# Decode attention on one core: softmax stages regrouped, and the scaled negative maximum moved from GpSimd to ScalarE

## The chip, the core and the metric

One Trainium2 chip, one core of it. The metric is the device time of one launch in microseconds (us); lower is better. The kernel before takes 512.92 us in the median of its first 5 runs (510.8 to 516.18). A run more than 1.5% above the fastest run of the same kernel counts as slow; everything compared below is fast unless said otherwise. Engines are named as the profile has them: PE (TensorE), DVE (VectorE), ACT (ScalarE), POOL (GpSimd), SP (SyncE, which here only issues DMAs).

## The reference

```python
B, H, Sq, Sk, D = 1, 16, 1, 8192, 256          # bf16 q, k, v
def reference(q, k, v):
    scale = q.shape[-1] ** -0.5
    scores = jnp.einsum("bhqd,bhkd->bhqk", q, k) * scale
    p = softmax(scores, axis=-1)
    return jnp.einsum("bhqk,bhkd->bhqd", p, v)
```

There is one query row per head. Each head reads 4 MiB of K and 4 MiB of V once, 134 MB in all, and does very little arithmetic on them.

## The kernel before

A head's 8192 keys lie on 128 partitions, 64 chunks each. K comes in 4 tiles of 16 chunks (1 MiB each), and so does V; 8 buffers for each, all issued from one queue. For each K tile, VectorE multiplies 7 chunks by q in one instruction and ScalarE sums them; the other 9 chunks VectorE multiplies and sums itself. Then comes the softmax over the head, and PE multiplies by V one head later.

```python
for h in range(H):
    for t in range(NKT):                        # 4 tiles of a head
        kt = kpool.tile([P, C, D], BF16, name="kt")
        k_eng.dma_start(out=kt, in_=kh[:, t * C : (t + 1) * C, :])
        nc.vector.tensor_tensor(out=prod[:], in0=kt[:, 0:BC, :], in1=..., op=ALU.mult)   # BC = 7
        for c in range(BC):                     # ScalarE sums a chunk
            nc.scalar.activation(out=junk, in_=prod[:, c, :], func=ACT.Copy,
                                 accum_out=scores[:, n0 + c : n0 + c + 1])
        for c in range(BC, C):                  # VectorE: multiply and sum a chunk
            nc.vector.tensor_tensor_reduce(out=scratch, in0=kt[:, c, :], in1=q_bc[:, h, :], ...,
                                           accum_out=scores[:, n : n + 1])
    nc.vector.tensor_reduce(out=rowmax, in_=scores, axis=AX.X, op=ALU.max)
    nc.gpsimd.partition_all_reduce(gmax, rowmax, channels=P, reduce_op=bass_isa.ReduceOp.max)
    nc.gpsimd.tensor_scalar(out=negbias, in0=gmax, scalar1=-scale, scalar2=None, op0=ALU.mult)
    nc.scalar.activation(out=p_h, in_=scores, func=ACT.Exp, bias=negbias, scale=scale,
                         accum_out=rowsum)
    nc.gpsimd.partition_all_reduce(den, rowsum, channels=P, reduce_op=bass_isa.ReduceOp.add)
    nc.vector.reciprocal(out=rden[0:1, :], in_=den[0:1, :])
    ...                                         # V loads, PE and scaling of the head before
```

The framework's scheduler orders the instructions of each engine when the program is built. In the traces an engine does not pass over one that waits: in the kernel before, VectorE is idle for 16.08 us before the reciprocal at 225.77 us, although the reductions behind it belong to a K tile whose multiply had already run at 208.26. So where an instruction stands on its engine has to be read from the built program, not from the source.

Of the kernel before, what the change touches and what calls it, by code (L numbers as in the profile page):

```python
# [8 lines left out]
FP32 = mybir.dt.float32  # L9
BF16 = mybir.dt.bfloat16  # L10
ACT = mybir.ActivationFunctionType
ALU = mybir.AluOpType
AX = mybir.AxisListType
# [3 lines left out]
def kernel(  # L17
# [7 lines left out]
    nc = tc.nc  # L25
    P = nc.NUM_PARTITIONS

    B, H, SQ, D = q.shape
# [3 lines left out]
    NCH = SK // P  # L32
    scale = float(D) ** -0.5

    C = min(int(os.environ.get("KC", "16")), NCH)
    VC = min(int(os.environ.get("VC", str(C))), NCH)
    assert NCH % C == 0 and NCH % VC == 0
    NKT = NCH // C
    NVT = NCH // VC
    BC_LIST = [int(x) for x in os.environ.get("BC", "7").split(",")]  # L40
# [2 lines left out]
    v_eng_name = os.environ.get("VENG", "sync")  # L43
    k_eng_name = os.environ.get("KENG", "sync")
    R = int(os.environ.get("RETIME", "2"))
    JUNK_PSUM = os.environ.get("JUNK_PSUM", "0") == "1"
    NORM_ENG = os.environ.get("NORM_ENG", "scalar")
    VLAG = int(os.environ.get("VLAG", "1"))
    QSPLIT = os.environ.get("QSPLIT", "1") == "1"

    q_flat = q.rearrange("b h q d -> (b h q d)")
    out_flat = out.rearrange("b h q d -> (b q) (h d)")

    consts = ctx.enter_context(tc.tile_pool(name="consts", bufs=1))
# [1 line left out]
    vpool = ctx.enter_context(tc.tile_pool(name="vpool", bufs=vbufs))  # L56
    ppool = ctx.enter_context(tc.tile_pool(name="ppool", bufs=3))
    junkp = ctx.enter_context(tc.tile_pool(name="junkp", bufs=2))
    small = ctx.enter_context(tc.tile_pool(name="small", bufs=6))
    spool = ctx.enter_context(tc.tile_pool(name="spool", bufs=5))  # L60
    scratch_pool = ctx.enter_context(tc.tile_pool(name="scratchp", bufs=2))
    psum_o = ctx.enter_context(tc.tile_pool(name="psum_o", bufs=R + 1, space=bass.MemoryType.PSUM))
    if JUNK_PSUM:
        psum_j = ctx.enter_context(tc.tile_pool(name="psum_j", bufs=2, space=bass.MemoryType.PSUM))

    v_eng = getattr(nc, v_eng_name)
    k_eng = getattr(nc, k_eng_name)
    norm_eng = getattr(nc, NORM_ENG)

    q_bc = consts.tile([P, H, D], BF16, name="q_bc")  # L70
    if QSPLIT:
        q2 = q.rearrange("b h q d -> (b q) h d")
        nc.sync.dma_start(out=q_bc[:, 0:1, :], in_=q2[:, 0:1, :].partition_broadcast(P))
        nc.gpsimd.dma_start(out=q_bc[:, 1:, :], in_=q2[:, 1:, :].partition_broadcast(P))  # L74
    else:
        nc.sync.dma_start(out=q_bc, in_=q_flat.partition_broadcast(P))

    ostage = consts.tile([1, H * D], BF16, name="ostage")

    o_tiles = {}  # L80
    p_tiles = {}
    rden_tiles = {}
    v_tiles = {}

    def issue_v(hh):
        vhh = v[0, hh].rearrange("(p n) d -> p n d", p=P)
        tiles = []
        for t in range(NVT):
            vt = vpool.tile([P, VC, D], BF16, name="vt")
            v_eng.dma_start(out=vt, in_=vhh[:, t * VC : (t + 1) * VC, :])  # L90
            tiles.append(vt)
        v_tiles[hh] = tiles

    def emit_norm(hh):
        o_ps = o_tiles.pop(hh)
        rden = rden_tiles.pop(hh)
        if NORM_ENG == "scalar":
            nc.scalar.activation(  # L98
                out=ostage[:, hh * D : (hh + 1) * D],
                in_=o_ps,  # L100
                func=ACT.Copy,
                scale=rden[0:1, 0:1],
            )
        else:
            nc.vector.tensor_scalar_mul(
                out=ostage[:, hh * D : (hh + 1) * D], in0=o_ps, scalar1=rden[0:1, 0:1]
            )

    for h in range(H):
        kh = k[0, h].rearrange("(p n) d -> p n d", p=P)  # L110
        vh = v[0, h].rearrange("(p n) d -> p n d", p=P)

        scores = spool.tile([P, NCH], FP32, name="scores")
        if VLAG == 0:
            pending_v_issue = h
        else:
            pending_v_issue = None
        for t in range(NKT):
            BC = min(BC_LIST[(h * NKT + t) % len(BC_LIST)], C)
            kt = kpool.tile([P, C, D], BF16, name="kt")  # L120
            k_eng.dma_start(out=kt, in_=kh[:, t * C : (t + 1) * C, :])  # L121
            n0 = t * C
            if BC > 0:
                prod = ppool.tile([P, BC, D], BF16, name="prod")
                nc.vector.tensor_tensor(  # L125
                    out=prod[:],
                    in0=kt[:, 0:BC, :],
                    in1=q_bc[:, h : h + 1, :].to_broadcast([P, BC, D]),
                    op=ALU.mult,
                )  # L130
                for c in range(BC):
                    if JUNK_PSUM:
                        junk = psum_j.tile([P, D], BF16, name="junkps")
                    else:
                        junk = junkp.tile([P, D], BF16, name="junk")
                    nc.scalar.activation(  # L136
                        out=junk,
                        in_=prod[:, c, :],
                        func=ACT.Copy,
                        accum_out=scores[:, n0 + c : n0 + c + 1],  # L140
                    )
            for c in range(BC, C):
                n = n0 + c
                scratch = scratch_pool.tile([P, D], BF16, name="scratch")
                nc.vector.tensor_tensor_reduce(  # L145
                    out=scratch,
                    in0=kt[:, c, :],
                    in1=q_bc[:, h, :],
                    scale=1.0,
                    scalar=0.0,  # L150
                    op0=ALU.mult,
                    op1=ALU.add,
                    accum_out=scores[:, n : n + 1],
                )

        rowmax = small.tile([P, 1], FP32, name="rowmax")
        nc.vector.tensor_reduce(out=rowmax, in_=scores, axis=AX.X, op=ALU.max)  # L157
        gmax = small.tile([P, 1], FP32, name="gmax")
        nc.gpsimd.partition_all_reduce(gmax, rowmax, channels=P, reduce_op=bass_isa.ReduceOp.max)  # L159
        negbias = small.tile([P, 1], FP32, name="negbias")  # L160
        nc.gpsimd.tensor_scalar(  # L161
            out=negbias, in0=gmax, scalar1=-scale, scalar2=None, op0=ALU.mult
        )

        p_h = spool.tile([P, NCH], BF16, name="p_h")
        rowsum = small.tile([P, 1], FP32, name="rowsum")
        nc.scalar.activation(  # L167
            out=p_h,
            in_=scores,
            func=ACT.Exp,  # L170
            bias=negbias,
            scale=scale,
            accum_out=rowsum,
        )
        den = small.tile([P, 1], FP32, name="den")
        nc.gpsimd.partition_all_reduce(den, rowsum, channels=P, reduce_op=bass_isa.ReduceOp.add)  # L176
        rden = small.tile([P, 1], FP32, name="rden")
        nc.vector.reciprocal(out=rden[0:1, :], in_=den[0:1, :])  # L178
        rden_tiles[h] = rden

        if VLAG == 0:
            issue_v(h)
        elif h - VLAG >= 0:
            issue_v(h - VLAG)

        def emit_pv(hp):
            o_ps = psum_o.tile([1, D], FP32, name="o_ps")
            o_tiles[hp] = o_ps
            p_use = p_tiles.pop(hp)
            tiles = v_tiles.pop(hp)  # L190
            for t in range(NVT):
                vt = tiles[t]
                for c in range(VC):
                    n = t * VC + c
                    nc.tensor.matmul(  # L195
                        out=o_ps,
                        lhsT=p_use[:, n : n + 1],
                        rhs=vt[:, c, :],
                        start=(n == 0),
                        stop=(n == NCH - 1),  # L200
                    )

        p_tiles[h] = p_h
        if VLAG == 0:
            emit_pv(h)
        elif h - VLAG >= 0:
            emit_pv(h - VLAG)

        if h - R - VLAG >= 0:
            emit_norm(h - R - VLAG)  # L210

    for hh in sorted(list(p_tiles.keys())):
        issue_v(hh)
        o_ps = psum_o.tile([1, D], FP32, name="o_ps")
        o_tiles[hh] = o_ps
        p_use = p_tiles.pop(hh)
        tiles = v_tiles.pop(hh)
        for t in range(NVT):
            vt = tiles[t]
            for c in range(VC):  # L220
                n = t * VC + c
                nc.tensor.matmul(  # L222
                    out=o_ps,
                    lhsT=p_use[:, n : n + 1],
                    rhs=vt[:, c, :],
                    start=(n == 0),
                    stop=(n == NCH - 1),
                )
    for hh in sorted(list(o_tiles.keys())):
        emit_norm(hh)  # L230

    nc.sync.dma_start(out=out_flat, in_=ostage)

# [29 lines left out]
```

## Time and profile before

| | before |
|---|---|
| time, median | 512.92 us |
| busy: DVE / ACT / PE / POOL | 53% / 39% / 29% / 6% |
| mean DMA rate over the span (first to last instruction) / from 12.76 to 90 us | 266 / 421 GB/s |
| DVE idle, waiting for `den` | 224.6 us in 16 waits |

The page's engine line, and its rows of 40 equal slices of the span (one digit is a busy share in tenths; GB/s is what the DMA engines moved), of the kernel before:

```profile
PE 150.1 (29%) x1024; PEld 99.1 (19%) x1024; DVE 269.1 (53%) x1248; ACT 196.5 (39%) x945; POOL 28.3 (6%) x53
...
DVE  3998272480934808439075191661925709357440
...
DMA  8999999986593874928839469284692864971000
GB/s 299 424 420 422 417 422 423 369 310 281 173 406 121 313 306 164 378 117 298 361 123 365 170 253 405 92 358 209 222 421 98 315 262 168 402 258 80 0 0 2
```

No engine is busy all the time. DMA is full from the second slice to the eighth and ragged after that, so something stops feeding it. The waits view (who waited for whom: total us, number of waits, longest) of the kernel before names it:

```profile
DVE rden L178 <- POOL den L176: 224.6, 16, 16.1
ACT p_h L167 <- POOL negbias L161: 190.4, 16, 15.5
...
POOL negbias L161 <- issue: 170.2, 16, 13.5
...
DVE prod L125 <- DMA kt<-in_k_dram: 8.8, 2, 8.3
```

VectorE loses 224.6 us, 14 us per head, to one 1x1 reciprocal, because its instructions run in order: everything behind the reciprocal waits too. It hardly ever waits for K (8.8 us, of which 8.3 at the start). Here is one head in the timeline of the kernel before (start, duration, engine, line, operation; in brackets the idle time of the engine and what ended it), cut to the softmax chain:

```profile
204.01 0.22 DVE L157 TENSOR_REDUCE rowmax<-scores 128x1 f32<-128x64 f32 x1
...
204.34 1.13 POOL L159 PARTITION_ALL_REDUCE gmax<-rowmax  x1 [11.60 <-DVE rowmax L157]
...
216.43 0.26 POOL L161 TENSOR_SCALAR negbias<-gmax 128x1 f32<-128x1 f32 x1 [10.97 <-issue]
216.73 0.35 ACT L167 ACTIVATE p_h<-scores,negbias 128x64 bf16<-128x64 f32 x1 [12.94 <-POOL negbias L161]
...
225.34 0.40 POOL L176 PARTITION_ALL_REDUCE den<-rowsum  x1 [8.64 <-issue]
225.77 0.15 DVE L178 RECIPROCAL rden<-den 1x1 f32<-1x1 f32 x1 [16.08 <-POOL den L176]
```

The arithmetic of this chain is about 2.5 us; it takes 21.9. The rest is two gaps on GpSimd of 10.97 and 8.64 us, "issue" in the profile: GpSimd waits for nothing that is recorded. At the start of each such gap the trace has a pair of MODIFY_POOL_CONFIG records, in all 32 gaps of the run (5.89 to 13.52 us long), and the built program has a library load there. We read this as an exchange of GpSimd's library, the all-reduce and tensor_scalar being in different ones (the trace names no library); such an exchange is called a swap below.

### The profile page before, as it was taken

The page shows a single profiled execution, that of the slowest core. Times are in us where ns is not written, and L with a number is a line of the kernel's source. Part 1 is how long each engine was busy: PE and PEld are TensorE (multiplying, and loading weights), DVE is VectorE, ACT ScalarE, POOL GpSimd, SP SyncE. Part 2 cuts the span into 40 slices and gives each one's busy share as a digit, 9 for nine tenths or more (in the row PEclk, how much of TensorE's full clock was granted, in tenths as well). Part 3 has the DMA queues.
Part 4 walks back from the last instruction along what each step waited for, and adds up shares of the span by engine and source line. Part 5 has one row for each costly group of instructions (what it writes and reads, how often), then busy time and mean ns, then how long its engine had stood idle before and what let it go on. Part 6 is the DMA issues. An engine that isn't in the chain of part 4 may idle for free.

```text
span 510.3 us, 4746 instructions
## 1 busy us (share of the span) xinstructions
PE 150.1 (29%) x1024; PEld 99.1 (19%) x1024; DVE 269.1 (53%) x1248; ACT 196.5 (39%) x945; POOL 28.3 (6%) x53
## 2 busy tenths in 40 slices
PE   0015522405107043070320702507006043070707
PEld 0013311303004022040220401304004022040504
DVE  3998272480934808439075191661925709357440
ACT  3663532424405344044441442414406244062620
POOL 0001010000000000100000000000000000001000
PEclk9998565956757557575585765756758557575758
DMA  8999999986593874928839469284692864971000
GB/s 299 424 420 422 417 422 423 369 310 281 173 406 121 313 306 164 378 117 298 361 123 365 170 253 405 92 358 209 222 421 98 315 262 168 402 258 80 0 0 2
DMA packets 18751, 135.59 MB, mean 266 GB/s; under 512 B 2081, under 2 KB 2209, under 8 KB 2337
## 3 DMA queue, kind: packets, MB, share of 16 engines
q1 hardware_dynamic: 18578, 134.30, 66.2%
q0 software_dynamic: 144, 0.98, 0.5%
q8 instruction: 8, 0.13, 0.1%
q14 instruction: 21, 0.17, 0.1%
HBM read 135.27 MB, written 0.01 MB: 265 GB/s over the span
## 4 chain that ended last, share of the span: by engine, by line
issue 37%; DVE 35%; ACT 18%; POOL 5%; DMA 2%; PE 2%; POOLq 0%; SPq 0%; DVEq 0%; ACTq 0%
DVE scratch L145 26%; ACT junk L136 16%; DVE prod L125 7%; POOL gmax L159 3%; DMA kt<-in_k_dram 2%; PE o_ps L222 2%; ACT p_h L167 1%; POOL den L176 1%; ACT ostage L98 1%; DVE scores L145 1%; POOL negbias L161 1%; DVE rowmax L157 1%; DVE rden L178 0%; POOLq L161 0%; SPq L121 0%
## 5 line engine op out<-in xcount | busy, mean ns | idle before, releaser
L195 PE MATMUL o_ps<-vt,p_h 128*1 128x256 bf16 x960 | 140.9, 322 | 341.7 <-ACT p_h L167 341.7
L136 ACT ACTIVATE junk<-prod 128x256 bf16<-128x256 bf16 x448 | 179.0, 400 | 107.5 <-DVE prod L125 106.0
L145 DVE CUSTOM_DVE_ANT_0 scratch<-kt,q_bc 128x256 bf16<-128x256 bf16 x576 | 204.2, 411 | 0.0
L195 PEld LDWEIGHTS <-p_h 128*1 128x1 bf16 x960 | 93.1, 98 | 389.3 <-ACT p_h L167 345.8
L178 DVE RECIPROCAL rden<-den 1x1 f32<-1x1 f32 x16 | 2.4, 151 | 224.6 <-POOL den L176 224.6
L136 ACT ACTIVATION_READ_ACCUMULATOR junk<-prod 128x1 f32 x448 | 83.2, 186 | 0.0
L167 ACT ACTIVATE p_h<-scores,negbias 128x64 bf16<-128x64 f32 x16 | 5.6, 348 | 190.4 <-POOL negbias L161 190.4
L125 DVE TENSOR_TENSOR prod<-kt,q_bc 128x1792 bf16<-128x1792 bf16 x64 | 69.1, 1080 | 8.8 <-DMA kt<-in_k_dram 8.8
L145 DVE DVE_READ_ACCUMULATOR2_ANT scores<- 128x1 f32 x576 | 42.9, 74 | 0.0
L159 POOL PARTITION_ALL_REDUCE gmax<-rowmax x16 | 16.6, 1037 | 184.1 <-DVE rowmax L157 184.1
L222 PE MATMUL o_ps<-vt,p_h 128*1 128x256 bf16 x64 | 9.2, 316 | 15.6 <-ACT p_h L167 15.6
L161 POOL TENSOR_SCALAR negbias<-gmax 128x1 f32<-128x1 f32 x16 | 4.2, 261 | 170.2 <-issue 170.2
L176 POOL PARTITION_ALL_REDUCE den<-rowsum x16 | 6.4, 402 | 120.3 <-issue 73.9
L98 ACT ACTIVATE ostage<-o_ps,rden 1x256 bf16<-1x256 f32 x16 | 7.2, 451 | 12.8 <-PE o_ps L222 8.9
L222 PEld LDWEIGHTS <-p_h 128*1 128x1 bf16 x64 | 6.1, 96 | 18.6 <-ACT p_h L167 15.9
L157 DVE TENSOR_REDUCE rowmax<-scores 128x1 f32<-128x64 f32 x16 | 3.5, 219 | 1.5
L167 ACT ACTIVATION_READ_ACCUMULATOR p_h<-scores,negbias 128x1 f32 x16 | 3.0, 186 | 0.0
L136 ACT ACT_TABLE_LOAD x1 | 1.3, 1283 | 0.7 <-PEq L247 0.7
L74 POOL DMA_DIRECT2D q_bc<-in_q_dram x1 | 0.9, 859 | 0.8 <-POOLq L247 0.8
L247 POOL MEMSET const-float32-0.0<- 128x1 f32 x1 | 0.1, 99 | 0.2 <-issue 0.2
L247 POOL MEMSET const-bfloat16-1.0<- 128x1 bf16 x1 | 0.1, 103 | 0.0
L247 POOL MEMSET const-uint8-127<- 128x1 uint8 x1 | 0.1, 102 | 0.0
(1 smaller groups left out, 0.1 us busy)
## 6 DMA issues: line engine op xcount, KB each, us to landing
kt<-in_k_dram SPq DMA_DIRECT2D x64, 1024.0 KB, 5.2
vt<-in_v_dram SPq DMA_DIRECT2D x64, 1024.0 KB, 11.5
q_bc<-in_q_dram POOLq DMA_DIRECT2D x1, 960.0 KB, 12.0
q_bc<-in_q_dram SPq DMA_DIRECT2D x1, 64.0 KB, 4.3
out_dram<-ostage SPq DMA_DIRECT2D x1, 8.0 KB
```

What stands on the lines that cost most here:

```text
L98: nc.scalar.activation(out=ostage[:, hh * D : (hh + 1) * D], in_=o_ps, func=ACT.Copy, scale=rden[0:1, 0:1],)
L125: nc.vector.tensor_tensor(out=prod[:], in0=kt[:, 0:BC, :], in1=q_bc[:, h : h + 1, :].to_broadcast([P, BC, D]), op=ALU.mult,)
L136: nc.scalar.activation(out=junk, in_=prod[:, c, :], func=ACT.Copy, accum_out=scores[:, n0 + c : n0 + c + 1],)
L145: nc.vector.tensor_tensor_reduce(out=scratch, in0=kt[:, c, :], in1=q_bc[:, h, :], scale=1.0, scalar=0.0, op0=ALU.mult, op1=ALU.add, accum_ ...
L157: nc.vector.tensor_reduce(out=rowmax, in_=scores, axis=AX.X, op=ALU.max)
L159: nc.gpsimd.partition_all_reduce(gmax, rowmax, channels=P, reduce_op=bass_isa.ReduceOp.max)
L161: nc.gpsimd.tensor_scalar(out=negbias, in0=gmax, scalar1=-scale, scalar2=None, op0=ALU.mult)
L167: nc.scalar.activation(out=p_h, in_=scores, func=ACT.Exp, bias=negbias, scale=scale, accum_out=rowsum,)
L176: nc.gpsimd.partition_all_reduce(den, rowsum, channels=P, reduce_op=bass_isa.ReduceOp.add)
L178: nc.vector.reciprocal(out=rden[0:1, :], in_=den[0:1, :])
L195: nc.tensor.matmul(out=o_ps, lhsT=p_use[:, n : n + 1], rhs=vt[:, c, :], start=(n == 0), stop=(n == NCH - 1),)
L222: nc.tensor.matmul(out=o_ps, lhsT=p_use[:, n : n + 1], rhs=vt[:, c, :], start=(n == 0), stop=(n == NCH - 1),)
```

## The change

The intent was to spread the softmax stages of a head over the next head's K tiles (max after tile 1, exp after tile 2, den after tile 3), so that the engines' lists do not stop for them. Besides, `negbias` moves to ScalarE, a few pools get one or two more buffers, and the loop is rewritten as stages. The core of the diff (cut; K tile work, V loads, matmuls and scaling are the same):

```diff
-        nc.gpsimd.tensor_scalar(
-            out=negbias, in0=gmax, scalar1=-scale, scalar2=None, op0=ALU.mult
-        )
+        nc.scalar.activation(out=negbias, in_=gmax, func=ACT.Copy, scale=-scale)
 ...
-    small = ctx.enter_context(tc.tile_pool(name="small", bufs=6))
-    spool = ctx.enter_context(tc.tile_pool(name="spool", bufs=5))
+    small = ctx.enter_context(tc.tile_pool(name="small", bufs=8))
+    spool = ctx.enter_context(tc.tile_pool(name="spool", bufs=6))
 ...
+    for h in range(H):
+        kh, scores = stage_k(h)
+        for t in range(NKT):
+            emit_ktile(h, t, kh, scores)
+            if t == min(T1, NKT - 1):
+                try_emit("max", h - 1)
+            if t == min(T2, NKT - 1):
+                try_emit("exp", h - 1)
+            if t == min(T3, NKT - 1):
+                try_emit("den", h - 1)
+        hv = h - 1 - VLAG                     # VLAG 1 -> 0: V and PE still one head behind
+        try_emit("vissue", hv)
+        try_emit("pv", hv)
+        try_emit("norm", hv - R)
```

What the scheduler makes of it on VectorE, from the built programs (T is the multiply that opens a K tile, MAX is rowmax, REC the reciprocal; the heads in the middle, all alike):

```
before:  T T MAX T T REC   T T MAX T T REC   ...
after:   T T T T MAX REC   T T T T MAX REC   ...
```

So the built program after the change does not stagger: rowmax and the reciprocal stand next to each other, with the whole chain between them. The kernel before has one whole tile and the opening of a second between them (a multiply and one reduction), 5.5 us of VectorE's work.

More of the change, by code (lines that the diff above doesn't have):

```diff
@@ L45 @@
     R = int(os.environ.get("RETIME", "2"))
-    JUNK_PSUM = os.environ.get("JUNK_PSUM", "0") == "1"
+    VLAG = int(os.environ.get("VLAG", "0"))
     NORM_ENG = os.environ.get("NORM_ENG", "scalar")
-    VLAG = int(os.environ.get("VLAG", "1"))
     QSPLIT = os.environ.get("QSPLIT", "1") == "1"
-    q_flat = q.rearrange("b h q d -> (b h q d)")
+    T1 = int(os.environ.get("T1", "1"))
+    T2 = int(os.environ.get("T2", "2"))
+    T3 = int(os.environ.get("T3", "3"))
+    q2 = q.rearrange("b h q d -> (b q) h d")
     out_flat = out.rearrange("b h q d -> (b q) (h d)")
@@ L58 @@
     junkp = ctx.enter_context(tc.tile_pool(name="junkp", bufs=2))
-    small = ctx.enter_context(tc.tile_pool(name="small", bufs=6))
-    spool = ctx.enter_context(tc.tile_pool(name="spool", bufs=5))
+    small = ctx.enter_context(tc.tile_pool(name="small", bufs=8))
+    spool = ctx.enter_context(tc.tile_pool(name="spool", bufs=6))
     scratch_pool = ctx.enter_context(tc.tile_pool(name="scratchp", bufs=2))
-    psum_o = ctx.enter_context(tc.tile_pool(name="psum_o", bufs=R + 1, space=bass.MemoryType.PSUM))
-    if JUNK_PSUM:
-        psum_j = ctx.enter_context(tc.tile_pool(name="psum_j", bufs=2, space=bass.MemoryType.PSUM))
+    psum_o = ctx.enter_context(tc.tile_pool(name="psum_o", bufs=R + 2, space=bass.MemoryType.PSUM))
     v_eng = getattr(nc, v_eng_name)
     k_eng = getattr(nc, k_eng_name)
-    norm_eng = getattr(nc, NORM_ENG)
     q_bc = consts.tile([P, H, D], BF16, name="q_bc")
     if QSPLIT:
-        q2 = q.rearrange("b h q d -> (b q) h d")
         nc.sync.dma_start(out=q_bc[:, 0:1, :], in_=q2[:, 0:1, :].partition_broadcast(P))
@@ L75, with stage_k @@
     else:
-        nc.sync.dma_start(out=q_bc, in_=q_flat.partition_broadcast(P))
+        nc.sync.dma_start(out=q_bc, in_=q2.partition_broadcast(P))
     ostage = consts.tile([1, H * D], BF16, name="ostage")
-    o_tiles = {}
-    p_tiles = {}
-    rden_tiles = {}
-    v_tiles = {}
-    def issue_v(hh):
-        vhh = v[0, hh].rearrange("(p n) d -> p n d", p=P)
+    st = {}
+    def stage_k(h):
+        kh = k[0, h].rearrange("(p n) d -> p n d", p=P)
+        scores = spool.tile([P, NCH], FP32, name="scores")
+        st[h] = dict(scores=scores)
+        tiles = []
+        return kh, scores
@@ new lines, in emit_ktile @@
+    def emit_ktile(h, t, kh, scores):
+        BC = min(BC_LIST[(h * NKT + t) % len(BC_LIST)], C)
+        kt = kpool.tile([P, C, D], BF16, name="kt")
+        k_eng.dma_start(out=kt, in_=kh[:, t * C : (t + 1) * C, :])
+        n0 = t * C
+        if BC > 0:
+            prod = ppool.tile([P, BC, D], BF16, name="prod")
+            nc.vector.tensor_tensor(
+                out=prod[:],
+                in0=kt[:, 0:BC, :],
+                in1=q_bc[:, h : h + 1, :].to_broadcast([P, BC, D]),
+                op=ALU.mult,
+            )
+            for c in range(BC):
+                junk = junkp.tile([P, D], BF16, name="junk")
+                nc.scalar.activation(
+                    out=junk,
+                    in_=prod[:, c, :],
+                    func=ACT.Copy,
+                    accum_out=scores[:, n0 + c : n0 + c + 1],
+                )
+        for c in range(BC, C):
+            n = n0 + c
+            scratch = scratch_pool.tile([P, D], BF16, name="scratch")
+            nc.vector.tensor_tensor_reduce(
+                out=scratch,
+                in0=kt[:, c, :],
+                in1=q_bc[:, h, :],
+                scale=1.0,
+                scalar=0.0,
+                op0=ALU.mult,
+                op1=ALU.add,
+                accum_out=scores[:, n : n + 1],
+            )
@@ new lines, in stage_max @@
+    def stage_max(h):
+        s = st[h]
+        rowmax = small.tile([P, 1], FP32, name="rowmax")
+        nc.vector.tensor_reduce(out=rowmax, in_=s["scores"], axis=AX.X, op=ALU.max)
+        gmax = small.tile([P, 1], FP32, name="gmax")
+        nc.gpsimd.partition_all_reduce(gmax, rowmax, channels=P, reduce_op=bass_isa.ReduceOp.max)
+        negbias = small.tile([P, 1], FP32, name="negbias")
+        nc.scalar.activation(out=negbias, in_=gmax, func=ACT.Copy, scale=-scale)
+        s["negbias"] = negbias
@@ new lines, in stage_exp, with stage_den @@
+    def stage_exp(h):
+        s = st[h]
+        p_h = spool.tile([P, NCH], BF16, name="p_h")
+        rowsum = small.tile([P, 1], FP32, name="rowsum")
+        nc.scalar.activation(
+            out=p_h,
+            in_=s["scores"],
+            func=ACT.Exp,
+            bias=s["negbias"],
+            scale=scale,
+            accum_out=rowsum,
+        )
+        s["p"] = p_h
+        s["rowsum"] = rowsum
+        del s["scores"]
+        del s["negbias"]
+    def stage_den(h):
+        s = st[h]
+        den = small.tile([P, 1], FP32, name="den")
+        nc.gpsimd.partition_all_reduce(den, s["rowsum"], channels=P, reduce_op=bass_isa.ReduceOp.add)
+        rden = small.tile([P, 1], FP32, name="rden")
+        nc.vector.reciprocal(out=rden[0:1, :], in_=den[0:1, :])
+        s["rden"] = rden
+        del s["rowsum"]
@@ L87, in issue_v, with stage_vissue @@
+    def stage_vissue(h):
+        vhh = v[0, h].rearrange("(p n) d -> p n d", p=P)
         tiles = []
@@ L91, in issue_v @@
             tiles.append(vt)
-        v_tiles[hh] = tiles
-    def emit_norm(hh):
-        o_ps = o_tiles.pop(hh)
-        rden = rden_tiles.pop(hh)
-        if NORM_ENG == "scalar":
-            nc.scalar.activation(
-                out=ostage[:, hh * D : (hh + 1) * D],
-                in_=o_ps,
-                func=ACT.Copy,
-                scale=rden[0:1, 0:1],
-            )
-        else:
-            nc.vector.tensor_scalar_mul(
-                out=ostage[:, hh * D : (hh + 1) * D], in0=o_ps, scalar1=rden[0:1, 0:1]
-            )
@@ L109 @@
-    for h in range(H):
-        kh = k[0, h].rearrange("(p n) d -> p n d", p=P)
-        vh = v[0, h].rearrange("(p n) d -> p n d", p=P)
-        scores = spool.tile([P, NCH], FP32, name="scores")
-        if VLAG == 0:
-            pending_v_issue = h
-        else:
-            pending_v_issue = None
-        for t in range(NKT):
-            BC = min(BC_LIST[(h * NKT + t) % len(BC_LIST)], C)
-            kt = kpool.tile([P, C, D], BF16, name="kt")
-            k_eng.dma_start(out=kt, in_=kh[:, t * C : (t + 1) * C, :])
-            n0 = t * C
-            if BC > 0:
-                prod = ppool.tile([P, BC, D], BF16, name="prod")
-                nc.vector.tensor_tensor(
-                    out=prod[:],
-                    in0=kt[:, 0:BC, :],
-                    in1=q_bc[:, h : h + 1, :].to_broadcast([P, BC, D]),
-                    op=ALU.mult,
-                )
-                for c in range(BC):
-                    if JUNK_PSUM:
-                        junk = psum_j.tile([P, D], BF16, name="junkps")
-                    else:
-                        junk = junkp.tile([P, D], BF16, name="junk")
-                    nc.scalar.activation(
-                        out=junk,
-                        in_=prod[:, c, :],
-                        func=ACT.Copy,
-                        accum_out=scores[:, n0 + c : n0 + c + 1],
-                    )
-            for c in range(BC, C):
-                n = n0 + c
-                scratch = scratch_pool.tile([P, D], BF16, name="scratch")
-                nc.vector.tensor_tensor_reduce(
-                    out=scratch,
-                    in0=kt[:, c, :],
-                    in1=q_bc[:, h, :],
-                    scale=1.0,
-                    scalar=0.0,
-                    op0=ALU.mult,
-                    op1=ALU.add,
-                    accum_out=scores[:, n : n + 1],
-                )
-        rowmax = small.tile([P, 1], FP32, name="rowmax")
-        nc.vector.tensor_reduce(out=rowmax, in_=scores, axis=AX.X, op=ALU.max)
-        gmax = small.tile([P, 1], FP32, name="gmax")
-        nc.gpsimd.partition_all_reduce(gmax, rowmax, channels=P, reduce_op=bass_isa.ReduceOp.max)
-        negbias = small.tile([P, 1], FP32, name="negbias")
-        nc.gpsimd.tensor_scalar(
-            out=negbias, in0=gmax, scalar1=-scale, scalar2=None, op0=ALU.mult
-        )
-        p_h = spool.tile([P, NCH], BF16, name="p_h")
-        rowsum = small.tile([P, 1], FP32, name="rowsum")
-        nc.scalar.activation(
-            out=p_h,
-            in_=scores,
-            func=ACT.Exp,
-            bias=negbias,
-            scale=scale,
-            accum_out=rowsum,
-        )
-        den = small.tile([P, 1], FP32, name="den")
-        nc.gpsimd.partition_all_reduce(den, rowsum, channels=P, reduce_op=bass_isa.ReduceOp.add)
-        rden = small.tile([P, 1], FP32, name="rden")
-        nc.vector.reciprocal(out=rden[0:1, :], in_=den[0:1, :])
-        rden_tiles[h] = rden
-        if VLAG == 0:
-            issue_v(h)
-        elif h - VLAG >= 0:
-            issue_v(h - VLAG)
-        def emit_pv(hp):
-            o_ps = psum_o.tile([1, D], FP32, name="o_ps")
-            o_tiles[hp] = o_ps
-            p_use = p_tiles.pop(hp)
-            tiles = v_tiles.pop(hp)
-            for t in range(NVT):
-                vt = tiles[t]
-                for c in range(VC):
-                    n = t * VC + c
-                    nc.tensor.matmul(
-                        out=o_ps,
-                        lhsT=p_use[:, n : n + 1],
-                        rhs=vt[:, c, :],
-                        start=(n == 0),
-                        stop=(n == NCH - 1),
-                    )
-        p_tiles[h] = p_h
-        if VLAG == 0:
-            emit_pv(h)
-        elif h - VLAG >= 0:
-            emit_pv(h - VLAG)
-        if h - R - VLAG >= 0:
-            emit_norm(h - R - VLAG)
@@ L212, with stage_pv @@
-    for hh in sorted(list(p_tiles.keys())):
-        issue_v(hh)
+        st[h]["vtiles"] = tiles
+    def stage_pv(h):
+        s = st[h]
         o_ps = psum_o.tile([1, D], FP32, name="o_ps")
-        o_tiles[hh] = o_ps
-        p_use = p_tiles.pop(hh)
-        tiles = v_tiles.pop(hh)
+        s["o_ps"] = o_ps
+        p_use = s["p"]
+        tiles = s.pop("vtiles")
         for t in range(NVT):
@@ L228, with stage_norm @@
                 )
-    for hh in sorted(list(o_tiles.keys())):
-        emit_norm(hh)
+        del s["p"]
+    def stage_norm(h):
+        s = st[h]
+        o_ps = s.pop("o_ps")
+        rden = s.pop("rden")
+        if NORM_ENG == "scalar":
+            nc.scalar.activation(
+                out=ostage[:, h * D : (h + 1) * D],
+                in_=o_ps,
+                func=ACT.Copy,
+                scale=rden[0:1, 0:1],
+            )
+        else:
+            nc.vector.tensor_scalar_mul(
+                out=ostage[:, h * D : (h + 1) * D], in0=o_ps, scalar1=rden[0:1, 0:1]
+            )
@@ new lines, with try_emit @@
+    done = {"max": -1, "exp": -1, "den": -1, "vissue": -1, "pv": -1, "norm": -1}
+    def try_emit(name, h):
+        if h < 0 or h >= H or h <= done[name]:
+            return
+        pred = {"max": None, "exp": "max", "den": "exp", "vissue": None, "pv": "vissue", "norm": "pv"}
+        if name == "pv":
+            for hh in range(done["exp"] + 1, h + 1):
+                try_emit("exp", hh)
+        pr = pred[name]
+        if pr is not None:
+            for hh in range(done[pr] + 1, h + 1):
+                try_emit(pr, hh)
+        for hh in range(done[name] + 1, h + 1):
+            if name == "max":
+                stage_max(hh)
+            elif name == "exp":
+                stage_exp(hh)
+            elif name == "den":
+                stage_den(hh)
+            elif name == "vissue":
+                stage_vissue(hh)
+            elif name == "pv":
+                stage_pv(hh)
+            elif name == "norm":
+                for h3 in range(done["den"] + 1, hh + 1):
+                    try_emit("den", h3)
+                stage_norm(hh)
+            done[name] = hh
@@ new lines @@
+    for h in range(H):
[12 more added lines that the diff above has]
+        try_emit("norm", hv - R)
+    try_emit("max", H - 1)
@@ L232 @@
+    try_emit("exp", H - 1)
+    try_emit("den", H - 1)
+    try_emit("vissue", H - 1)
+    try_emit("pv", H - 1)
+    try_emit("norm", H - 1)
     nc.sync.dma_start(out=out_flat, in_=ostage)
```

## The prediction

> **What bounds the kernel now.** The page's engine table shows no engine full: VectorE (DVE) 269 us busy (53%), ScalarE (ACT) 197, PE 150. The DMA row is full (421 GB/s) for the first 90 us, then ragged: 265 GB/s over the span. The waits view names the loss: VectorE waits 224.6 us in 16 waits for the reciprocal `rden` <- GpSimd `den`, about 14 us per head. The timeline of the head at 204 us shows why: rowmax 204.0; gmax all-reduce ends 205.5; then GpSimd shows 10.97 us of "issue" before the 0.26 us `negbias`; Exp 216.7 to 217.2; again 8.64 us of issue before the 0.40 us `den` (225.3); the reciprocal at 225.8 ends a 16.1 us idle of the in-order VectorE. The 32 issue gaps each hold a MODIFY_POOL_CONFIG: alternating partition_all_reduce and tensor_scalar on GpSimd swaps its library twice per head. [...] those under DMA load are 7 to 13 us. One head takes about 32.5 us: 4 tiles x 4.11 us of VectorE = 16.5, plus that stall.
>
> **What the change does.** It moves `negbias` (16 x 0.26 us) from GpSimd to ScalarE (an estimated 0.25 us each). The built order has a single GpSimd library load, so all 32 swaps, some 9 us each, go. Sizes, tiles, work per head, buffers of K and V are the same; the DMA order too. The advertised staggering (max/exp/den between the next head's tiles) is not what the built order shows: from head 2 on, VectorE runs four tiles, then rowmax and the reciprocal back to back, so VectorE still waits for the whole softmax chain; only the chain is short. Estimate from trace pieces: 0.1 + 0.33 (rowmax to gmax) + 0.37 (gmax when VectorE is idle, as for the last head; it is 1.13 only beside a `prod` multiply) + 0.3 negbias + 0.5 Exp + 0.45 den + 0.15 = about 2.2 us. VectorE per head: 16.5 + 2.2 = 18.7 us.
>
> **The new limit.** 8.39 MB per head at 421 GB/s is 19.9 us, more than VectorE's 18.7, ScalarE's 12.5 and PE's 9.7. So the kernel becomes bound by DMA. [...] this trace sustains 421, so I use 421. Sum: the first 12.76 us move 3.8 MB (299 GB/s); the other 131.5 MB take 312 us: last V tile at 325. Then 16 matmuls 2.4, norm 0.5, output and end 2.4 (as in the old tail): span about 330, timed time 2 more: **332 us** (range 327 to 345). If the chain were over 3.4 us, VectorE would pace: 1 us per head more is about +16 us, plus a 10 us PV tail after the last head, some 350.
>
> Chances: faster by over 2% 0.985, same 0.01, slower 0.005.
>
> **What the profile would show.** Right: the DMA row at 9 and about 421 GB/s until some 325 us; MODIFY_POOL_CONFIG gone but once; VectorE's wait for `den` about 2 us per head (30 to 35 us in all); VectorE waiting about 1 us per head for `kt`; one head every 20 us. Wrong: ragged DMA row, VectorE without waits for `kt`, den waits of 4 us or more.
>
> **What would make it wrong.** The all-reduce having hidden cost behind its rough spans; ScalarE reaching negbias late; K or V issues stuck behind each other in the single queue; DMA slowing under fuller engines; PE's clock, granted about 0.6, falling so far that PV lags V.

12.76 us for the first 3.8 MB and 312 us for the other 131.5 MB at the 421 GB/s of the trace give 325, the 5.3 us of the tail some 330, and 2 us more the 332.

## The result and the profile after

The kernel after takes 341.06 us (median of 8 runs, 340.94 to 341.14), beside 512.34 us of the kernel before in the same rounds. The ratio is 0.6651, 95% interval 0.6633 to 0.6669. A ratio is computed as the mean time of one kernel's fast runs over that of the other's of the same rounds, so it is not quite the ratio of the medians. The prediction was 332 us with a range of 327 to 345: the measured time lies in the range, 9 us above the number.

The page's engine line and rows of the kernel after:

```profile
PE 150.9 (45%) x1024; PEld 100.0 (30%) x1024; DVE 270.4 (80%) x1248; ACT 204.2 (60%) x961; POOL 13.8 (4%) x37
...
DVE  0999989797969969697795969959599795979900
...
DMA  6999999999999999999999999999999999999940
GB/s 239 428 423 423 420 420 423 421 419 423 423 419 419 422 422 421 419 422 420 424 423 416 421 423 422 420 418 425 420 420 422 424 416 422 423 420 417 423 181 11
```

DMA is now full at about 421 GB/s from the second slice to the last but two. The waits view of the kernel after:

```profile
PE o_ps L177 <- DMA vt<-in_v_dram: 80.6, 13, 11.5
...
DVE rden L154 <- POOL den L152: 26.9, 15, 1.9
DVE prod L94 <- DMA kt<-in_k_dram: 25.9, 13, 8.1
ACT negbias L129 <- POOL gmax L127: 15.8, 16, 1.5
```

VectorE's wait for `den` went from 224.6 to 26.9 us, and it now waits for K: 25.9 us in 13 waits, 8.1 of them at the start. The timeline of one head of the kernel after, cut to the chain and the next head's first multiply:

```profile
200.26 0.22 DVE L125 TENSOR_REDUCE rowmax<-scores 128x1 f32<-128x64 f32 x1
200.65 0.35 POOL L127 PARTITION_ALL_REDUCE gmax<-rowmax  x1 [19.14 <-DVE rowmax L125]
201.03 0.20 ACT L129 ACTIVATE negbias<-gmax 128x1 f32<-128x1 f32 x1 [0.99 <-POOL gmax L127]
...
201.27 0.35 ACT L136 ACTIVATE p_h<-scores,negbias 128x64 bf16<-128x64 f32 x1
...
201.87 0.38 POOL L152 PARTITION_ALL_REDUCE den<-rowsum  x1 [0.87 <-ACT p_h L136]
202.29 0.15 DVE L154 RECIPROCAL rden<-den 1x1 f32<-1x1 f32 x1 [1.81 <-POOL den L152]
...
203.48 1.09 DVE L94 TENSOR_TENSOR prod<-kt,q_bc 128x1792 bf16<-128x1792 bf16 x1 [1.04 <-DMA kt<-in_k_dram]
```

From rowmax to the end of the reciprocal it is 2.18 us, and then VectorE is idle for 1.04 us because its K tile has not come. The 32 pairs of MODIFY_POOL_CONFIG in the gaps are gone; one pair, at 2.2 us, is left. gmax, which took 1.13 us in the middle of the kernel before, takes 0.35: before, a K tile's multiply ran beside it on VectorE; now VectorE is idle then. (The one all-reduce of the kernel after that does run beside a multiply, the first, takes 1.12.)

The 9 us that the prediction did not have show at the end of the run. The windows view (busy us of each engine in stretches of the span; at the end of a line the granted clock, the DMA share and GB/s) of the kernel after:

```profile
306.00:322.00 16.00, 5.30 (x29) 3.27 (x29) 16.00 (x75) 11.41 (x55) 0.00 (x0) 0.57 1.02 421
322.00:326.00 4.00, 4.00 (x38) 2.98 (x36) 0.68 (x4) 0.84 (x5) 0.73 (x2) 1.00 0.75 313
326.00:330.00 4.00, 2.91 (x26) 2.06 (x25) 0.00 (x0) 0.46 (x1) 0.00 (x0) 1.00 0.12 49
330.00:334.00 4.00, 2.90 (x26) 1.96 (x25) 0.00 (x0) 0.00 (x0) 0.00 (x0) 1.00 0.07 27
```

The rate does not fall from 421 to 0. From 326 us on, 49 and then 27 GB/s still flow for 8 us. One DMA engine's share of 421 GB/s is 26: one or two of the 16 engines are late, the others have finished. In the trace each tile's semaphore is counted up 16 times, which we take as once by each DMA engine, and the tile is used only after the last: the multiply at 203.48 us above starts 0.03 us after the last count-up of its tile and 2.57 us after the 15th. So the lag can be read. Worked out from them, in us (this is not a view of the profile):

```
kernel after       first of 16   8th      14th     15th     last     last - first
5th K tile            18.49      18.83    19.64    19.92    20.30     1.81
last tile            323.89     325.71   326.96   329.68   333.95    10.06
steps of the last engine (a tile more than 0.25 us later than its pace of 2.48 us):
  at  53.0 +0.46   60.9 +0.44   81.3 +0.46  114.5 +0.99  145.3 +0.98
     181.1 +0.97  211.9 +0.97  242.6 +0.94  275.9 +0.90  309.2 +0.99      sum 8.1
DMA packets of the kind "instruction", 8192 bytes, one series among several, start at
      49.7          79.2         110.9        142.9
     178.1         209.5         240.9        274.4         306.8
```

One engine falls behind, from 110 us on in steps of just under 1 us each 31 to 36 us, and each step but one shows in a tile that lands 1.5 to 3.6 us after a packet of this series (by its kind it brings instructions). (The one at 60.9 comes 4.1 us after a packet of 16384 bytes of the same kind.) The largest delay of the 16 sets the time, not the mean rate.

### The profile page after: what moved, and what is told of

Its sections match the earlier page's. It is cut to its first block, busy times and chain, and to the rows that moved or that the text cites. A ratio compares the mean times of both kernels' runs of the same rounds, so it can differ in the third digit from the quotient of the medians.

```text
span 338.8 us, 4696 instructions
## 1 busy us (share of the span) xinstructions
PE 150.9 (45%) x1024; PEld 100.0 (30%) x1024; DVE 270.4 (80%) x1248; ACT 204.2 (60%) x961; POOL 13.8 (4%) x37
## 4 chain that ended last, share of the span: by engine, by line
DMA 75%; DVE 21%; issue 1%; POOL 1%; ACT 1%; PE 1%; SPq 0%; DVEq 0%
DMA kt<-in_k_dram 70%; DVE scratch L111 15%; DMA vt<-in_v_dram 6%; DVE prod L94 5%; PE o_ps L177 1%; DVE scores L111 1%; POOL den L152 0%; ACT p_h L136 0%; POOL gmax L127 0%; DVE rowmax L125 0%; ACT negbias L129 0%; SPq L90 0%; DVE rden L154 0%; ACT ostage L191 0%; SPq L71 0%
## 5 line engine op out<-in xcount | busy, mean ns | idle before, releaser
L94 DVE TENSOR_TENSOR prod<-kt,q_bc 128x1792 bf16<-128x1792 bf16 x64 | 69.4, 1085 | 25.9 <-DMA kt<-in_k_dram 25.9
L111 DVE DVE_READ_ACCUMULATOR2_ANT scores<- 128x1 f32 x576 | 46.0, 80 | 0.0
L154 DVE RECIPROCAL rden<-den 1x1 f32<-1x1 f32 x16 | 2.4, 151 | 26.9 <-POOL den L152 26.9
L127 POOL PARTITION_ALL_REDUCE gmax<-rowmax x16 | 6.4, 398 | 295.4 <-DVE rowmax L125 295.4
L129 ACT ACTIVATE negbias<-gmax 128x1 f32<-128x1 f32 x16 | 3.2, 203 | 15.8 <-POOL gmax L127 15.8
```

The source lines that it names most:

```text
L129: nc.scalar.activation(out=negbias, in_=gmax, func=ACT.Copy, scale=-scale)
```

## The experiments

The theory: (1) the two GpSimd library swaps per head, on the chain that VectorE waits for, are the whole loss of the kernel before; (2) without them DMA is the limit; (3) the limit is the slowest of 16 DMA engines, and what slows it is VectorE's own instruction stream, fetched over it (a conjecture from the steps and packets just shown, which runs 3 to 5 test). The rivals: the staging or the pools bring the gain; VectorE (80% busy) is the limit; the late DMA engine is slow by itself. Three groups of runs, each with runs of the kernel before on the same chip (medians 513.1, 513.24 and 513.78 us). All results were correct.

### 1. The kernel before, with `negbias` on ScalarE and nothing else

```diff
-        nc.gpsimd.tensor_scalar(
-            out=negbias, in0=gmax, scalar1=-scale, scalar2=None, op0=ALU.mult
-        )
+        nc.scalar.activation(out=negbias, in_=gmax, func=ACT.Copy, scale=-scale)
```

> The kernel before with one edit: negbias computed on ScalarE, nothing else of the change. Theory (the GpSimd library swaps on the softmax chain are the whole loss; without them the kernel is DMA-bound): 339 to 344 us, like the kernel after (341.06). Rival (the staged emission, larger pools and later V issue bring the gain): stays well above, 400 us or more.

Measured: 341.2 us (4 runs, 341.17 to 341.69), ratio 0.6654 (0.6635 to 0.6673); the kernel after has 0.6651. The waits view of this run has, for VectorE and its reciprocal:

```profile
DVE rden L176 <- POOL den L174: 27.5, 16, 1.9
```

Compare 224.6 and 26.9. One line is the whole gain; the staged emission, the larger pools and the rest of the rewrite add nothing that can be measured. The built order is also the same in the middle heads, T T T T MAX REC: the scheduler changed the order with the line, so this run does not separate the two. But the order cannot be what gains, because the old one gave VectorE more work beside the chain (5.5 us), not less; what fell is the chain, by the swaps.

### 2. The kernel after, with `negbias` back on GpSimd

The same edit the other way round. Its built order is one that really staggers, with four tiles between a head's rowmax and its reciprocal: `MAX T T T T REC  MAX T T T T REC`.

> The kernel after with one edit: negbias back on GpSimd. The built order of this one does stagger (rowmax of a head, four tiles of the next head, then the reciprocal), so VectorE has 16.5 us of work beside the chain. Theory: the swap chain itself (about 1.1 + 11 + 0.5 + 8.6 + 0.4 + handover, some 22 us) now paces the heads, 16 x 22 to 23 us plus start and tail: 370 to 400 us, far above 341 and below 512. Rival (staging alone gives the gain): 341 to 345 us. Rival (staging gives nothing): 505 to 515 us.

Measured: 419.03 us (417.09 and 420.97), ratio 0.8169. The restructuring (staging, pools and V issue together) is worth 94 us here, and the library swaps cost 78 us over the kernel after in spite of it. It is 19 us above the range that was expected. The GpSimd timeline of this run shows one head:

```profile
199.86 1.13 POOL L127 PARTITION_ALL_REDUCE gmax<-rowmax  x1 [2.92 <-DVE rowmax L125]
212.41 0.26 POOL L129 TENSOR_SCALAR negbias<-gmax 128x1 f32<-128x1 f32 x1 [11.42 <-issue]
221.37 0.40 POOL L154 PARTITION_ALL_REDUCE den<-rowsum  x1 [8.71 <-ACT junk L102]
225.00 1.13 POOL L127 PARTITION_ALL_REDUCE gmax<-rowmax  x1 [3.23 <-DVE rowmax L125]
```

gmax to den is 21.9 us, as expected; but the next gmax does not follow at once, so the head takes 25.1 us, not 22 to 23. The waits view of this run says what was left out:

```profile
ACT p_h L138 <- POOL negbias L129: 188.2, 16, 16.6
...
DVE rowmax L125 <- ACT junk L102: 37.8, 14, 4.1
```

ScalarE also runs in order: while it waits 188 us for `negbias`, it does not sum the next head's chunks, so that head's rowmax then waits for ScalarE (2.7 us in each of 14 heads).

### 3. Is VectorE the limit? Nine chunks per tile on ScalarE

```diff
-    BC_LIST = ... "7"
+    BC_LIST = ... "9"
```

> The kernel after with 9 of 16 chunks per tile reduced on ScalarE in place of 7. VectorE loses 4 x (2 x 0.345 - 0.28) = about 1.6 us per head, 26 us in all, and a fifth of its instructions (994 rows in place of 1250); ScalarE gains 3.2 us per head and 256 instructions. Theory (DMA paces): 338 to 342 us, the small rest from fewer VectorE instruction fetches and more of ScalarE. Rival (VectorE paces): 315 to 325 us.

Measured: 339.19 us (4 runs, 339.14 to 339.23). VectorE's busy time falls from 270.4 to 243.0 us, and the time by 1.9. The waits view shows where the freed time went:

```profile
DVE prod L94 <- DMA kt<-in_k_dram: 30.2, 13, 8.1
...
DVE rowmax L125 <- ACT junk L102: 24.0, 15, 4.0
```

VectorE waits longer for K (25.9 in the kernel after) and now for ScalarE's sums. It is not the limit. The last tile landed at 332.17 us (333.95 in the kernel after), with 8.17 us between its first and last engine (10.06).

### 4. Fewer instructions on VectorE, same arithmetic and bytes

On top of run 3, the 7 chunks left to VectorE take two instructions instead of 14.

```diff
-        for c in range(BC, C):
-            nc.vector.tensor_tensor_reduce(out=scratch, in0=kt[:, c, :], in1=q_bc[:, h, :], ...,
-                                           accum_out=scores[:, n : n + 1])
+        nc.vector.tensor_tensor(out=rest[:], in0=kt[:, BC:C, :],
+                                in1=q_bc[:, h : h + 1, :].to_broadcast([P, C - BC, D]), op=ALU.mult)
+        nc.vector.tensor_reduce(out=scores[:, n0 + BC : n0 + C], in_=rest, axis=AX.X, op=ALU.add)
```

> As the run with 9 chunks on ScalarE, and VectorE does the other 7 by one multiply and one row reduction, not by 7 fused instructions with their read-outs: 226 VectorE rows in place of 1250, about the same VectorE time as the kernel after. Theory (the DMA engine that carries VectorE's instruction fetches loses 1 us per 8 KB fetch, and the slowest of the 16 engines sets when each tile lands): the 10 VectorE fetches become 2; the spread of a tile's 16 landings at the end falls from 10 us to 6 to 8 us (the engine with ScalarE's fetches, now 9 or 10, becomes the slowest), time 336 to 339.5 us. Rival (that engine is slow by itself, or the 1 us losses have another cause): the spread stays at 10 us, steps each 31 us, time 341.

Measured: 338.3 us (4 runs, 338.24 to 338.64), VectorE busy 278.1 us, more than in the kernel after. The end of this run in the windows view:

```profile
322.00:326.00 4.00, 3.83 (x34) 2.68 (x32) 0.15 (x1) 0.56 (x3) 0.38 (x1) 1.00 0.77 322
326.00:330.00 4.00, 3.00 (x27) 2.18 (x27) 0.00 (x0) 0.00 (x0) 0.00 (x0) 1.00 0.10 41
330.00:334.00 4.00, 2.71 (x24) 1.75 (x21) 0.00 (x0) 0.47 (x1) 0.00 (x0) 1.00 0.01 4
```

The straggling stretch is shorter: 4 GB/s, not 27, in the last of these. The spread of the last tile is 7.35 us, and one engine is late, not two (15th of 16 at 327.25 us, 329.68 in the kernel after). The steps of just under 1 us in the rhythm above are gone. What is left is one early step of 1.2 us at 58.8 us, 2.7 us after a packet of 16384 bytes, and steps of 0.65 to 0.79 us at 146.5, 179.6, 215.1, 245.6, 278.5 and 309.0 us; packets with instructions start at 143.5, 177.4, 211.8, 244.1, 275.5 and 305.7. ScalarE has 1217 instructions in this run, 961 in the kernel after. How many a packet holds can be estimated from the kernel after: another series of its 8192-byte packets starts at 64.8, 102.1, 142.8, 183.6, 224.3, 266.3 and 306.7 us, and from one to the next ScalarE has 115 to 121 instructions, 119 in the mean. If that series is ScalarE's, its 76 instructions per head of some 20.4 us need one packet each 32 us in this run (an estimate: 119 / 76 x 20.4), and 30.5 to 35.5 us are seen. So the late engine is now most likely the one that brings ScalarE's instructions. Runs 3 and 5, with the same 1217 ScalarE instructions, agree: there the second-last engine (the 15th) lands its part of the last tile at 331.32 us, which is where the last one lands here. With 961 it is 329.68 us in the kernel after (330.35 to 330.46 in its repeat, run 1 and the memset run of section 6).

### 5. More instructions on VectorE, same K and V

The kernel after once more as a yardstick, and run 3 with 384 one-element copies on VectorE, whose results nothing reads:

```diff
+            if c - BC < TINY:                 # TINY = 6 per tile
+                i = (h * NKT + t) * TINY + c - BC
+                nc.vector.tensor_copy(out=idle[:, i : i + 1], in_=kt[0:1, c, 0:1])
```

> The kernel after, unchanged, as the yardstick for this group of runs and for the chip-to-chip spread: 340.5 to 341.7 us.

> The run with 9 chunks on ScalarE (339.19 us) plus 384 one-element VectorE copies that nothing needs, 6 per tile, spread evenly: 1378 VectorE rows in place of 994, 3 more 8 KB fetches, some 1.7 us of VectorE time per head, which still leaves VectorE under the DMA pace of 20 us. No byte of K or V is added. Theory (each VectorE fetch costs the slowest DMA engine 0.95 to 1.0 us): last landing 2.5 to 3.5 us later, spread at the end 10.5 to 11.5 us in place of 8.2, steps every 30 us or so, time 341.5 to 343 us. Rival (instruction fetches have nothing to do with it): 339 us, spread 8.2.

Measured: the kernel after 341.02 us (4 runs, 340.94 to 341.12), so times of different groups can be compared to about 0.1 us. With the copies 342.19 us (341.94 to 342.33), 3.0 us above run 3. VectorE is still not the limit; its multiplies still wait for K in this run's groups view:

```profile
L96 DVE TENSOR_TENSOR prod<-kt,q_bc 128x2304 bf16<-128x2304 bf16 x64 | 86.0, 1344 | 18.1 <-DMA kt<-in_k_dram 18.1
L125 DVE COPY idle<-kt 1x1 bf16<-1x1 bf16 x384 | 53.5, 139 | 0.0
```

The runs that vary VectorE's instructions, side by side (landings from the semaphore count-ups):

```
                        DVE instructions   last - first   last tile landed   time
4. few instructions            224             7.35           331.32         338.3
3. nine chunks on ACT          992             8.17           332.17         339.19
   kernel after               1248            10.06           333.95         341.06
5. with idle copies           1376            11.21           334.94         342.19
```

(Instructions as the pages count them; the recorded texts have two more each.) Three more runs with 1248 VectorE instructions (the repeat, run 1 and the memset run of section 6) have their last landing at 333.98, 334.02 and 334.07 us, so it repeats to about 0.1 us. From run 3 to run 5 VectorE has 384 instructions more, and these are an estimated three packets: in the kernel after, VectorE has 112 to 145 instructions from one packet of the series shown with its result to the next, 124 in the mean (at which 1250 and 226 rows are also the 10 and 2 fetches of the expectation in section 4). The last landing moves by 2.77 us. Between run 3, the kernel after and run 5 the time goes in step with the number of VectorE instructions, though VectorE's busy time (243.0, 270.4 and 266.0 us) and the bytes of K and V do not. The rhythm follows too: in the later part of these runs the steps of the last engine come on average each 40.7, 32.4 and 29.9 us, which at a head per 20.4 us is about 125 VectorE instructions per step in all three. (In run 3 packets of 16384 bytes come at that rhythm as well, so its steps alone would not decide.) Run 4 lies above that line because another engine is then last. The rival, an engine slow by itself, is out: it would not follow a count of instructions. That the series of packets belong to VectorE and ScalarE is inferred from their rhythm and number (the trace does not say whose instructions a packet holds, nor which DMA engine took it). The packets themselves take 0.31 to 0.39 us in the kernel after, and a step is just under 1 us with VectorE's, about 0.7 with ScalarE's in run 4; why the loss is larger is not shown.

### 6. The library swap off the chain, and a control

The kernel after plus one unused GpSimd instruction per head: in the first run a tensor_scalar right after `den`, for which the program has the two library loads again; in the second a memset, for which it has none.

```diff
         nc.gpsimd.partition_all_reduce(den, s["rowsum"], ...)
+        nc.gpsimd.tensor_scalar(out=unused, in0=den, scalar1=-scale, scalar2=None, op0=ALU.mult)
```
```diff
         nc.vector.reciprocal(out=rden[0:1, :], in_=den[0:1, :])
+        nc.gpsimd.memset(den, 0.0)
```

> The kernel after plus one GpSimd tensor_scalar per head right after den, whose result nothing reads: the library is swapped twice per head as in the kernel before, but off the softmax chain, in the 18 us in which GpSimd is idle. If a swap back starts as soon as GpSimd reaches it, before gmax's data is there: 341 to 346 us, and swaps as such cost nothing. If it is paid only at the first call, after the wait for rowmax: gmax comes 6 to 11 us late in each head and VectorE paces: 430 to 500 us.

> Control for the run with a GpSimd tensor_scalar off the chain (437.9 us): the kernel after plus one GpSimd memset of the 128 values of den per head, after the reciprocal. It is as small as that tensor_scalar and stands at the same place, but the built program has no library load for it, and it reads nothing. Theory (the library swap, and VectorE holding off a GpSimd operation[...], were the cost): 340.5 to 342.5 us. Rival (any GpSimd operation between two all-reduces costs, by its place in the order or by contention): clearly over 345 us.

(A clause on which GpSimd operations are held off is cut from it, as no run here separates them by that. The holding off itself is in the trace of the run with the tensor_scalar, below.)

Measured: with the memset 341.23 us (341.15 and 341.3), so a GpSimd instruction such as this costs nothing by standing between `den` and the next `gmax`. (The memset needs no library load and also reads nothing, so this control does not say which of the two differences matters; the timeline below separates the swap from the rest of the delay.) With the tensor_scalar 431.7 us in its one fast run (the other, 444.04, was slow). That number falls into the range expected for a swap paid late, but the GpSimd timeline of this run shows another reason:

```profile
188.79 8.76 POOL L154 TENSOR_SCALAR unused<-den 128x1 f32<-128x1 f32 x1 [7.97 <-issue]
207.21 0.38 POOL L127 PARTITION_ALL_REDUCE gmax<-rowmax  x1 [9.65 <-issue]
...
244.90 0.45 POOL L154 TENSOR_SCALAR unused<-den 128x1 f32<-128x1 f32 x1 [7.71 <-issue]
254.29 0.38 POOL L127 PARTITION_ALL_REDUCE gmax<-rowmax  x1 [8.94 <-DVE rowmax L125]
```

and VectorE's timeline of the same run, for the first of these heads:

```profile
197.56 0.22 DVE L125 TENSOR_REDUCE rowmax<-scores 128x1 f32<-128x64 f32 x1
```

The unused tensor_scalar lasts 8.76 us. It ends at 197.55 us, and VectorE's rowmax starts at 197.56, after its last reduction. In 11 of the 16 heads it lasts 4.8 to 9.4 us and ends within 5 ns of a rowmax's start; in the other five it takes 0.26 to 0.46 us. So in these 11 heads it is held through a whole row of VectorE instructions that read K and q, not through one; what holds it is not in the trace. In three of the five short ones (at 45.55, 113.91 and 244.90 us) VectorE was in such a row too, and the tensor_scalar got through, ending about 0.1 us after the VectorE instruction that ran; what decides between the two is not shown. In the head at 188.79 the swap back begins only after the hold, at 197.86 us, and gmax starts 9.65 us after rowmax's start. The head at 244.90 was lucky: its tensor_scalar took 0.45 us, the swap back began at 245.66, well before rowmax at 253.93, and gmax started 0.36 us after rowmax's start, with no delay. So a swap back does not wait for the all-reduce's data; it can hide where the instruction between the swaps is not held up. Whether a swap could be hidden in every head was not tried.

### 7. A version that beats both

Run 4, plus two things that the DMA limit suggests: q is broadcast to the partitions by PE from an 8 KB load (ones times q into PSUM, the memory for PE's results; 8 matmuls) and no longer by 1.05 MB of broadcast loads; and the last V tile is loaded in four pieces, so that the last matmuls start earlier.

```diff
-        nc.sync.dma_start(out=q_bc[:, 0:1, :], in_=q2[:, 0:1, :].partition_broadcast(P))
-        nc.gpsimd.dma_start(out=q_bc[:, 1:, :], in_=q2[:, 1:, :].partition_broadcast(P))
+    for j in range(H * D // 512):
+        nc.tensor.matmul(out=q_ps, lhsT=ones, rhs=q_row[:, j * 512 : (j + 1) * 512], ...)
+        ...                                    # copied to q_bc by VectorE and ScalarE in turn
 ...
+                for i in range(0, VC, 4):      # last V tile of the last head only
+                    part = vend.tile([P, 4, D], BF16, name="part")
+                    v_eng.dma_start(out=part, in_=vhh[:, t * VC + i : t * VC + i + 4, :])
```

> The version with few VectorE instructions (338.3 us), with q broadcast to 128 partitions by TensorE from an 8 KB load in place of 1.05 MB of broadcast loads, and the last V tile loaded in four pieces. Theory (DMA-bound by the slowest of 16 engines): the 1.05 MB at 421 GB/s, 2.5 us, goes from the start (first K tile at some 5.7 us in place of 8.1), and 1.4 us of last matmuls go from the tail: 333.5 to 336 us. If the first tile's arrival does not move, 337 us.

Measured: 334.02 us (4 runs, 333.99 to 334.05), ratio 0.6513 (0.6484 to 0.6542). The first K tile's multiply starts at 6.08 us, and the last DMA is issued at 329.64 us. Of the 4.3 us gained over run 4, 3.3 are an earlier last landing (328.00 us, not 331.32) and 0.8 a shorter tail after it; the two changes were not run apart. This run has no DMA from GpSimd's queue at all, and its last piece of V still lands over 6.96 us.

## Why the prediction was right or wrong

- **What bounds the kernel before: right.** The library swaps on VectorE's in-order chain; run 1 edits nothing else and gets the whole gain. A gap is 5.9 to 7.2 us in the four where DMA is idle (the last two heads), and 7.9 to 13.5 us where it is full; each of the 32 changes from one operation to the other was paid again.
- **"The advertised staggering is not what the built order shows": right**, and run 2 adds that the one version that does stagger gains 94 us while the swaps are there.
- **VectorE per head, 18.7 us: right.** Measured from the first multiply to the end of the reciprocal: 183.61 to 202.44 us, 18.83. The chain was put at 2.2 us and is 2.18.
- **The new limit is DMA at about 421 GB/s: right** (run 3: 27 us of VectorE time taken away, 1.9 us gained). This program runs on one core, and its traces that are DMA-bound sustain about 421 for 300 us (in the kernel after 416 to 428 GB/s in each slice from the second to the last but two).
- **"Last V tile at 325": this step failed, by 9 us.** It divided the bytes by the mean rate. The fastest engine did finish at 323.9 us; but a tile has landed when the slowest of 16 has its part, and that one ended at 333.95. Of the 10.06 us between them 1.8 were there from the first tiles, and 8.1 came in steps. Seven of these, 6.7 us, have the rhythm that runs 3, 4 and 5 tie to the fetching of VectorE's instructions; the first three, 1.4 us, are less clear. One head therefore took 20.45 us (gmax at 200.65 to gmax at 302.90, five heads), not 19.9.
- **The tail after the last landing: right.** 5.3 us were put, 4.9 measured (333.95 to 338.8), and 2.3 us between span and timed time, where 2 were put.
- **What was to be seen:** den waits 30 to 35 us, measured 26.9; about 1 us of waiting for `kt` per head, measured 17.8 us in the 12 waits after the start; DMA full until some 325 us, which is right for 14 of the 16 engines.

## What to carry to other kernels

Where GpSimd alternates between two kinds of operation, as here between all-reduce and tensor_scalar, look for unexplained "issue" gaps beside MODIFY_POOL_CONFIG (5.9 to 13.5 us here), and move the small operation to another engine before restructuring anything: here one line gave 172 us and the restructuring nothing on top of it. When a kernel becomes DMA-bound, read the last landing and not the mean rate alone, because the slowest DMA engine can set the time, as here; there, fewer instructions on an engine can pay a little even if its busy time does not shrink (run 4 against run 3: 0.9 us of 339). And read the built order before believing what the source says about overlap.
